# Hedgehog attention, Fourier mixing and an FFN in one kernel: the DFT by symmetry with folded channels, row-tiled projections, layer-norm scale applied after the FFN, DMA transposes

## The chip, the cores and the metric

The kernel runs on one core of a Trainium2 chip. The metric is device time in microseconds (us). Executions of one kernel lie within about 1% of each other. Where two kernels are compared, their runs were taken on the same chip in turn.

## The reference, cut to what matters

For each of 8 batches: linear attention with an exponential feature map, then the real part of a two-dimensional DFT as a mixing layer, then a layer norm and an FFN.

```python
def phi(x):
    proj = einsum('bhsd,df->bhsf', x, w_phi)               # 64 -> 128 features
    proj = proj - max(abs(proj), axis=-1)
    return concatenate([exp(proj), exp(-proj)], axis=-1)
kv  = einsum('bhsf,bhsd->bhfd', phi(k), v);  z = sum(phi(k), axis=2)
x   = einsum('bhsf,bhfd->bhsd', phi(q), kv) / (phi(q) . z + 1e-6)   # 8 heads of 576 x 64
x   = heads side by side                                   # 576 x 512 per batch
u   = x + real(fft(fft(x, axis=1), axis=2))
un  = (u - mean(u)) / sqrt(var(u) + 1e-6)
out = u + relu(un @ w_ch1) @ w_ch2                         # 512 -> 2048 -> 512
```

## The kernel before

Each batch has three stages, and each loop turn writes the attention of batch b+1 ahead of mixing and FFN of batch b. What is interleaved with what is fixed when the program is built: in the four steady batches from 255 to 590 us the trace shows the same TensorE order from the mixing's last product to the FFN's first, with the numerators (`psnum`) of two heads in each.

```python
# attention, per head h (pr = h // 2; rr = the 64 partitions of this head)
nc.tensor.matmul(psqh[:, 0:512], lhsT=wphi2[rr, :], rhs=QT[rr, pr, 0:512], start=True, stop=True)
...                                                   # and columns 512 to 640
nc.scalar.activation(out=QPh_p[:], in_=psqh[:, 0:640], func=AT.Exp, scale=1.0)
nc.scalar.activation(out=QPh_n[:], in_=psqh[:, 0:640], func=AT.Exp, scale=-1.0)
...                                                   # psqs, pskk: 5 matmuls each; max |.| of both
...                                                   # KPp, KPn: exponentials; VSCp, VSCn: values scaled
for fh in range(2):
    KP, VSC = (KPp, VSCp) if fh == 0 else (KPn, VSCn)
    c0 = 640 + fh * (D + 1)
    for jj in range(NSC):                             # NSC = 5 tiles of 128 rows
        nc.tensor.matmul(pskk[:, c0: c0 + D + 1], lhsT=KP[:, jj, :], rhs=VSC[:, jj, :],
                         start=(jj == 0), stop=(jj == NSC - 1))
...                                                   # kvh copy, psnum: 10 matmuls, X on VectorE

# mixing, after the column means (pmb) and sums (pcs)
for cc in range(NCC):
    for term, (MAT, DST) in enumerate([(CS_r, DT), (SS_r, ET)]):
        for kb in range(2):
            ...
            for js in range(NSC):
                nc.tensor.matmul(psD[:, 0:288], lhsT=XF[0:M, js, 128 * cc: 128 * cc + 128],
                                 rhs=MAT[0:M, js, 288 * kb: 288 * kb + 288], ...)
...                                                   # psu: 40 matmuls of 512 columns; U = psu + X
# layer norm: bn_stats and bn_aggr of the 5 row tiles, then
for g0, g1 in [(0, 3), (3, NSC)]:
    ...                                               # 1/sqrt(var) in rstd, by three Newton steps
    for kk in range(g0, g1):
        nc.scalar.activation(out=UN[0:M, kk, :], in_=U[0:M, kk, :], func=AT.Identity,
                             bias=nbias[0:M, kk: kk + 1], scale=rstd[0:M, kk: kk + 1])
        pUT = get_psumB().tile([128, 512], BF16, tag="pb", name="pUT")
        ...                                           # 4 transposes on TensorE into pUT
        nc.vector.tensor_copy(out=UNT[:, :, 128 * kk: 128 * kk + M], in_=pUT_v[:, :, 0:M])
...                                                   # FFN: psh, 128 matmuls of 288; pso, 80 of 512
nc.vector.tensor_tensor(out=OUT[0:M, :], in0=pso[0:M, :], in1=U[0:M, kk, :], op=ALU.add)
nc.sync.dma_start(out=out[b, 128 * kk: 128 * kk + M, :], in_=OUT[0:M, :])

# loop
for i, b in enumerate(batches):
    ...
    Xs[nb] = attention_core(nb, staged.pop(nb))       # nb: the next batch
    fft_ffn(b, Xs.pop(b))
```

## Time and profile before

| | before |
|---|---|
| time | 892.06 us (891.19 to 892.93) |
| TensorE busy | 673.9 us, 75% of the profiled span of 893.2 |
| VectorE, ScalarE, GpSimd busy | 467.0, 420.9, 110.2 us |
| first mixing stage begins at | about 136 us |
| a steady batch | 100.5 us, TensorE busy 82 |

The page of the kernel before gives the shares of the chain that ended last and, in 40 equal slices of the span, TensorE's busy tenths and the clock that it was granted, in tenths:

```profile
PE 64%; ACT 11%; DVE 8%; DMA 6%; SPq 6%; issue 2%; POOL 2%; DVEq 0%; ACTq 0%; POOLq 0%
...
PE   0112439795996699795996699787996799699887
...
PEclk9999999877996889877996889878996899689989
```

TensorE carries the chain, with a dip to 6 or 7 tenths in the middle of every batch, where its clock falls too. It lies between the mixing's last product and the FFN's first. The first fence has the last products, from the timeline; the second goes on in the chain in order of time (start, duration, what, number of instructions):

```profile
368.34 0.62 PE L390 MATMUL psu<-SDn_r,ET 128*64 128x512 bf16 x2
```

### The profile page before, as it was taken

How to read it: one execution, taken by the hardware profiler on the slowest of the kernel's cores; microseconds unless marked ns; L12 is line 12 of the kernel's file. 1: busy time of each engine (PE TensorE's matmuls, PEld its weight loads, DVE VectorE, ACT ScalarE, POOL GpSimd, SP SyncE). 2: the span in 40 equal slices, each digit the busy share in tenths (PEclk: the TensorE clock that was granted, in tenths of full speed). 3: DMA queues.
4: the chain of work that ended last, by engine and by line, in shares of the span. 5: the costliest groups of instructions: out<-in, count | busy, mean ns of one | idle time of the engine just before them, and what ended most of it. 6: DMA issues, size and time to landing. Idle time of an engine off the chain costs nothing.

```text
span 893.2 us, 13139 instructions
## 1 busy us (share of the span) xinstructions
PE 673.9 (75%) x5000; PEld 391.1 (44%) x5032; DVE 467.0 (52%) x1366; ACT 420.9 (47%) x886; POOL 110.2 (12%) x140
## 2 busy tenths in 40 slices
PE   0112439795996699795996699787996799699887
PEld 0002324463454445363454445364544545364463
DVE  8575635851477316951477316960577237833411
ACT  2599434373255425373155425373256606470270
POOL 8710140014000320014000320010000000000000
PEclk9999999877996889877996889878996899689989
DMA  9992190029100980029100980019100310001001
GB/s 99 147 196 19 32 107 1 1 30 110 54 1 1 93 82 18 1 27 113 54 2 1 90 85 18 1 26 73 43 1 1 59 54 1 1 1 48 6 1 53
DMA packets 164094, 39.15 MB, mean 44 GB/s; under 512 B 156864, under 2 KB 158912, under 8 KB 164032
## 3 DMA queue, kind: packets, MB, share of 16 engines
q0 software_dynamic: 115264, 18.39, 31.2%
q1 hardware_dynamic: 48768, 19.94, 10.9%
q8 instruction: 39, 0.64, 0.3%
q14 instruction: 23, 0.19, 0.1%
HBM read 36.77 MB, written 9.44 MB: 52 GB/s over the span
## 4 chain that ended last, share of the span: by engine, by line
PE 64%; ACT 11%; DVE 8%; DMA 6%; SPq 6%; issue 2%; POOL 2%; DVEq 0%; ACTq 0%; POOLq 0%
PE pso L486 16%; PE psh L474 12%; PE psD L361 12%; PE psu L385 4%; PE psu L390 3%; DMA VS<-in_v_dram 3%; SPq L195 3%; PE pskk L276 3%; SPq L196 3%; DMA QT<-QS 3%; PE pskk L235 3%; PE psqs L225 2%; PE psqh L210 2%; DVE MM L246 2%; PE psnum L290 2%
## 5 line engine op out<-in xcount | busy, mean ns | idle before, releaser
L474 PE MATMUL psh<-UNT,W1b 128*128 128x288 bf16 x1024 | 161.8, 320 | 16.7 <-ACT HT L481 16.7
L486 PE MATMUL pso<-W2b,HT 128*128 128x512 bf16 (+1 forms) x624 | 140.8, 380 | 0.8
L474 PEld LDWEIGHTS <-W1b 128*128 128x128 bf16 x1024 | 107.4, 109 | 57.9 <-issue 19.7
L481 ACT ACTIVATE HT<-psh 128x288 bf16<-128x288 f32 x256 | 97.9, 415 | 52.2 <-PE psh L474 46.0
L491 DVE TENSOR_TENSOR OUT<-pso,U 128x512 f32<-128x512 f32 (+1 forms) x40 | 27.6, 690 | 169.7 <-PE pso L486 169.7
L368 ACT CAST DT<-psD 128x288 bf16<-128x288 f32 x64 | 24.9, 404 | 155.2 <-PE psD L361 154.9
L486 PEld LDWEIGHTS <-HT 128*128 128x128 bf16 (+1 forms) x640 | 63.5, 100 | 73.5 <-issue 3.4
L276 PE MATMUL pskk<-VSCp,KPp 128*128 128x65 bf16 x320 | 23.4, 210 | 73.1 <-DVE VSCp L264 50.7
L361 PEld LDWEIGHTS <-XF 128*128 128x128 bf16 (+1 forms) x640 | 52.5, 98 | 55.3 <-issue 29.8
L243 DVE TENSOR_REDUCE MM<-psqs 128x5 f32<-128x640 f32 x64 | 52.7, 824 | 38.9 <-PE psqs L225 37.3
L220 ACT ACTIVATE QPhp<-psqh 128x640 bf16<-128x640 f32 x64 | 45.0, 704 | 53.3 <-PE psqh L214 48.5
L260 ACT ACTIVATE KPp<-pskk 128x640 bf16<-128x640 f32 x64 | 45.0, 702 | 52.2 <-DVE MM L246 39.0
L235 PE MATMUL pskk<-wphi,KT 64*128 64x128 bf16 x320 | 36.1, 248 | 39.8 <-DMA KT<-KS 38.1
L361 PE MATMUL psD<-CS_r,XF 128*128 128x288 bf16 (+1 forms) x320 | 62.8, 299 | 0.0
L361 PE MATMUL psD<-SS_r,XF 128*128 128x288 bf16 (+1 forms) x320 | 60.9, 298 | 0.0
L210 PE MATMUL psqh<-QT,wphi 64*128 64x512 bf16 x64 | 31.0, 484 | 39.4 <-DMA QT<-QS 29.7
L225 PE MATMUL psqs<-wphi,QT 64*128 64x128 bf16 x320 | 37.0, 258 | 25.8 <-ACT QPhn L221 21.1
L306 DVE TENSOR_TENSOR tmpg<-psnum,EE 128x325 f32<-128x325 f32 x64 | 31.7, 495 | 47.0 <-PE psnum L296 47.0
L276 PEld LDWEIGHTS <-KPp 128*128 128x128 bf16 x320 | 18.0, 107 | 87.0 <-ACT KPn L261 48.8
L246 DVE TENSOR_REDUCE MM<-pskk 128x5 f32<-128x640 f32 x64 | 52.0, 812 | 4.1 <-PE pskk L235 2.7
L173 POOL MEMSET VS<- 64x520 bf16 x8 | 4.5, 558 | 390.0 <-DVE VSCn L268 389.9
L225 PEld LDWEIGHTS <-QT 64*128 64x128 bf16 x320 | 24.5, 112 | 53.9 <-issue 33.8
(98 smaller groups left out, 1120.8 us busy)
## 6 DMA issues: line engine op xcount, KB each, us to landing
out_dram<-OUT SPq DMA_DIRECT2D x32, 256.0 KB, 2.0
QS<-in_q_dram POOLq DMA_DIRECT2D x32, 128.0 KB, 4.8
KS<-in_k_dram POOLq DMA_DIRECT2D x32, 128.0 KB, 4.7
VS<-in_v_dram POOLq DMA_DIRECT2D x32, 128.0 KB, 5.7
W1b<-in_moe_w_ch_dram POOLq DMA_DIRECT2D x1, 2048.0 KB, 14.6
W2b<-in_moe_w_ch_dram POOLq DMA_DIRECT2D x1, 2048.0 KB, 23.8
out_dram<-OUT SPq DMA_DIRECT2D x8, 128.0 KB, 2.3
QT<-QS SPq DMA_TRANSPOSE x40, 3.8
```

The source lines that it names most:

```text
L210: nc.tensor.matmul(psqh[:, 0:512], lhsT=wphi2[rr, :], rhs=QT[rr, pr, 0:512], start=True, stop=True,)
L220: nc.scalar.activation(out=QPh_p[:], in_=psqh[:, 0:640], func=AT.Exp, scale=1.0)
L225: nc.tensor.matmul(psqs_v[:, jj, :], lhsT=QT[rr, pr, 128 * jj: 128 * jj + 128], rhs=wphi2[rr, :], start=True, stop=True,)
L235: nc.tensor.matmul(pskk_v[:, jj, :], lhsT=KT[rr, pr, 128 * jj: 128 * jj + 128], rhs=wphi2[rr, :], start=True, stop=True,)
L243: nc.vector.tensor_reduce(out=MM[:, 0, :], in_=psqs_v, axis=AX.X, op=ALU.max, apply_absolute_value=True)
L246: nc.vector.tensor_reduce(out=MM[:, 1, :], in_=pskk_v, axis=AX.X, op=ALU.max, apply_absolute_value=True)
L260: nc.scalar.activation(out=KPp[:], in_=pskk_v, func=AT.Exp, scale=1.0)
L276: nc.tensor.matmul(pskk[:, c0: c0 + D + 1], lhsT=KP[:, jj, :], rhs=VSC[:, jj, :], start=(jj == 0), stop=(jj == NSC - 1),)
L361: nc.tensor.matmul(psD[:, 0:288], lhsT=XF[0:M, js, 128 * cc: 128 * cc + 128], rhs=MAT[0:M, js, 288 * kb: 288 * kb + 288], start=(js == 0), ...
L474: nc.tensor.matmul(psh[:, 0:288], lhsT=W1b[:, cc, 128 * hh: 128 * hh + 128], rhs=UNT[:, cc, 288 * hf: 288 * hf + 288], start=(cc == 0), st ...
L481: nc.scalar.activation(out=out_ap, in_=psh[:, 0:288], func=AT.Relu)
L486: nc.tensor.matmul(pso[0:M, :], lhsT=HT[:, hh, 128 * kk: 128 * kk + M], rhs=W2b[:, hh, :], start=(hh == 0), stop=(hh == NHH - 1),)
```

## The change

The intent was to take work from TensorE. The mixing of real rows has a symmetric result (row k at channel n equals row 576-k at channel 512-n), so half of the rows are computed and used twice; channels n and 512-n are added and subtracted first (`CE`, `CO`), so half of the channels are multiplied. Row 0 is subtracted from all rows, in place of the column means. Rows are loaded several to a descriptor, and projections go in pairs of 64-row tiles. The layer norm's mean is subtracted by GpSimd, a DMA transposes the result, and 1/sqrt multiplies the FFN's output, since ReLU lets a positive factor through. Cut to its core:

```diff
 # attention: 4 row tiles of 128 and, two heads to a tile, the last 64 rows
-                for jj in range(NSC):
-                    nc.tensor.matmul(
-                        pskk[:, c0: c0 + D + 1],
-                        lhsT=KP[:, jj, :],
-                        rhs=VSC[:, jj, :],
...
+                nc.tensor.matmul(
+                    kv[:, i, :], lhsT=K4[rr, pr, :], rhs=V4[rr, pr, :], start=True, stop=False
+                )
+                for j in range(4):
+                    nc.tensor.matmul(
+                        kv[:, i, :], lhsT=KP[:, h, j, :], rhs=VC[:, h, j, :],
+                        start=False, stop=(j == 3),
+                    )
...
 # mixing: row 0 subtracted, channels folded, half the rows
+        nc.vector.tensor_tensor(
+            out=XC[:, 0:4, 0:C], in0=X[:, 0:4, :],
+            in1=pm[:].unsqueeze(1).to_broadcast([128, 4, C]), op=ALU.subtract,
+        )
...
+        for sl in (slice(0, 2), slice(2, 4), slice(4, 5)):
+            for dst, op in ((CE, ALU.add), (CO, ALU.subtract)):
+                nc.gpsimd.tensor_tensor(
+                    out=dst[:, sl, :], in0=XC[:, sl, 0:256], in1=XC[:, sl, C:256:-1], op=op
+                )
...
+        for mt in range(2):
+            for src, mat, dst in ((CE, CS, DT), (CO, SS, ET)):
+                ps = pb.tile([128, NK], F32, tag="pb", name="psD")
+                for c in range(5):
+                    nc.tensor.matmul(
+                        ps[:], lhsT=src[:, c, 128 * mt:128 * mt + 128], rhs=mat[:, c, :],
...
 # layer norm
-                nc.scalar.activation(
-                    out=UN[0:M, kk, :], in_=U[0:M, kk, :], func=AT.Identity,
-                    bias=nbias[0:M, kk: kk + 1], scale=rstd[0:M, kk: kk + 1],
-                )
...
+            nc.gpsimd.tensor_scalar(
+                out=UN[0:M, c, :], in0=X[0:M, c, :], scalar1=mv[0:M, c, 0:1], scalar2=None,
+                op0=ALU.subtract,
+            )
+            nc.sync.dma_start_transpose(
+                out=UT[:, :, 128 * c:128 * c + M], in_=UN[0:M, c, :]
+            )
...
+                nc.vector.tensor_tensor(
+                    out=X[:, 2 + t, 1:C], in0=pu[:, C - 1:0:-1], in1=X[:, 2 + t, 1:C], op=ALU.add
+                )
...
 # FFN output
-            nc.vector.tensor_tensor(
-                out=OUT[0:M, :], in0=pso[0:M, :], in1=U[0:M, kk, :], op=ALU.add
-            )
+                nc.vector.scalar_tensor_tensor(
+                    out=O[0:M, :], in0=po[0:M, :], scalar=rs[0:M, c:c + 1], in1=U[0:M, c, :],
+                    op0=ALU.mult, op1=ALU.add,
+                )
...
 # loop
+    for b in range(B):
+        X = attention(b, loaded)
+        if b + 1 < B:
+            loaded = load(b + 1)
+        mixed = mixing(b, X)
+        if done is not None:
+            ffn(b - 1, *done)
+        done = mixed
+    ffn(B - 1, *done)
```

## The prediction

> **What bounds the kernel now.** I read the stages first, then the chain that ended last, then the groups. Stages (each engine's busy us in a stretch; PEclk is the granted clock, DMA the busy share of the 16 engines as the view scales it):
>
> ```profile
> 0.00:60.00 60.00, 6.67 (x46) 3.52 (x47) 43.95 (x133) 33.96 (x47) 37.66 (x51) 1.00 1.75 145
> 60.00:136.00 76.00, 29.13 (x268) 18.84 (x268) 41.26 (x119) 44.66 (x72) 15.42 (x19) 1.00 0.77 62
> ...
> 340.00:440.50 100.50, 82.19 (x627) 47.98 (x631) 52.68 (x155) 45.91 (x103) 13.09 (x16) 0.86 0.44 43
> ...
> 824.00:893.00 69.00, 60.09 (x347) 33.06 (x348) 17.19 (x56) 23.18 (x53) 0.00 (x0) 0.95 0.06 20
> ```
>
> So: 136 us pass before the first mixing stage; then a batch takes 95 to 102 us (here 340 to 440.5), with TensorE busy 82 of 100; a tail of 69. Inside that batch the chain is mostly TensorE in its own order:
>
> ```profile
> 412.54 1.90 ACT XB L325
> 415.32 4.87 PE psh L474 x28
> 420.45 10.74 PE pso L486 x49
> 431.25 3.09 PE pso L486 x13
> 434.33 1.29 PE pmb L330 x5
> 436.78 3.36 PE pso L486 x15
> 440.52 3.64 PE psD L361 x22
> ```
>
> and finer stretches show the two weak places, where TensorE waits for the attention's chain of VectorE and ScalarE (370 to 375), and for the next batch's transposes (397 to 413):
>
> ```profile
> 370.00:375.00 5.00, 1.33 (x20) 1.07 (x19) 4.75 (x24) 1.64 (x4) 0.00 (x0) 0.86 0.00 0
> ...
> 397.00:413.00 16.00, 8.32 (x77) 5.92 (x75) 3.94 (x13) 5.18 (x15) 6.40 (x8) 0.83 1.32 112
> ```
>
> The prologue is transfers (the DMA strip of the page stands at 9 tenths there; 156864 of 164094 packets under 512 B by the page) and table reloads: sines of the constants alternate with exponentials, and one head takes 20 us around 60 to 80 us.
>
> Dense work is best read at the end, with nothing beside it: psD 824.0 to 837.5 (13.5 us), psu to 846.2 (8.9), FFN 853.0 to 889 (36.0). These rows size the small work:
>
> ```profile
> L474 PE MATMUL psh<-UNT,W1b 128*128 128x288 bf16 x1024 | 161.8, 320 | 16.7 <-ACT HT L481 16.7
> ...
> L491 DVE TENSOR_TENSOR OUT<-pso,U 128x512 f32<-128x512 f32 (+1 forms) x40 | 27.6, 690 | 169.7 <-PE pso L486 169.7
> ...
> L243 DVE TENSOR_REDUCE MM<-psqs 128x5 f32<-128x640 f32 x64 | 52.7, 824 | 38.9 <-PE psqs L225 37.3
> L220 ACT ACTIVATE QPhp<-psqh 128x640 bf16<-128x640 f32 x64 | 45.0, 704 | 53.3 <-PE psqh L214 48.5
> ```
>
> (320 ns is a latency; the matmuls issue every 143 ns on average in that last FFN, 18.4 us for 128.)
>
> **What the Trainium skill says.** (1) "GPSIMD Engine Reference", section Performance versus the Vector engine: an fp32 two-operand add of 2048 columns takes 4497 ns on GpSimd and 2293 on VectorE. The trace agrees for VectorE: 495 ns at 325 columns and 690 at 512 give 1.04 ns a column, 2290 at 2048. It has no GpSimd arithmetic, so my GpSimd terms are estimates from this page: 2.2 ns a column plus some 0.1 us. (2) "TensorE: Matmul & The Clock Gate", Part 1: after idle windows of 3.4 us the array runs at half rate. The trace agrees: the ten psnum matmuls issue every 30 ns at 359 us, every 55 ns at 375 us (granted clock 0.50 from 375 to 380). (3) "ScalarE: Activation LUTs", What ACT_TABLE_LOAD costs: about 1283 ns; this trace has 1283.
>
> **The change part by part.** *Removed from TensorE per batch:* psD from 80 matmuls of 288 columns to 20 of 320: 13.5 to about 2.7 + 0.7 (the extra row px), psu from 40 to 12: 8.9 to 2.6. Mean and column-sum matmuls and transposes go (pmb 1.3, pcs 1.2, pUT about 2.2); one fp32 matmul for row 0 comes (some 1 us). Gain 13.5+8.9+4.7−7.0 = 20 us of TensorE. FFN (36) is unchanged; so are the 160 small kv and numerator matmuls. Projections stay 80 matmuls, in pairs of row tiles.
>
> *Prologue:* loads of 512 and 1024 B instead of 256; packets per batch fall from 13824 to 5632 (counted from the shapes), at the present 38.7 ns x packets / 16 engines that is 14 us. Only one batch is loaded ahead, and the constants need 28 VectorE steps instead of 126. But sines and exponentials still alternate in the built order. My sum for the first attention's end: data and transposes 20, key exponentials, sines and table loads 21, query part 12, heads 13: 66 us, against about 130.
>
> *The order is the risk.* The built order on TensorE is no longer interleaved. Each steady iteration is: heads(b), key projections(b+1), row 0 and mixing(b), FFN(b−1), query projections(b+1), heads(b+1). TensorE keeps this order, so it waits out each chain with only what stands before. I size the parts:
>
> - *D, query part after the FFN:* last output op 0.9; three reductions of 1024 columns at 1.22 (scaled from 824 ns at 640): 4.6; a small matmul and exponential 0.7; then eight exponentials of 1024 columns at 1.02 (from 704 at 640, 0.82 ns a column): 8.2, all ahead of the first kvh copy in ScalarE's order. 14 us, TensorE nearly idle, and cold.
> - *H, heads:* kv, copy, numerator, next kv: cold, 10 x 55 ns twice, 0.27 copy, 0.2 latency and two hand-offs: 1.65 x 8 = 13 us. VectorE's 1.2 a head fits below.
> - *B, mixing:* last tg, comb and rden with two key reductions between them 3.7; GpSimd's X 0.85; row-0 matmul 1.8; subtraction of 2048+512 columns on VectorE 2.9: centred rows at 9.3. GpSimd meanwhile has V4 twice, two load issues at 0.87 and four V products at 1.2 ahead of the fold, so it is free only at 12.4. Fold: copy 0.2, six sums 6.1, corner repair 1.6: 20.3. psD 4.6 (cold), copies 0.7, psu 4 to 5: FFN may start at 29.5.
> - *C, FFN:* 36, plus 2 because three psu buffers of the shared pool of three come free only as VectorE adds and normalises.
>
> Sum of a steady batch: 14+13+29.5+38 = 94.5, against 95 to 102. So the 20 us taken from TensorE come back as idle time of TensorE: I expect 2 to 7 us a batch from the steady state and the rest from the prologue.
>
> Whole: 66 + B(0) 30 + 5 (there no FFN hides the normalisation) + 7 x 94.5 = 662, less 7 for the last mixing (no next batch on GpSimd) + last FFN 36 + output tail 4 (as now, 889 to 893) = 796; call it 800.
>
> *LN scale on the output, DMA transposes:* UN's transposes leave TensorE, ScalarE and VectorE; five DMA transposes of 1.25 us issue each (present issue time of a 128x512) have a whole iteration to land. Key and query transposes follow the query part: 5.9 + 5.9 us of issue and some 2.5 to land, ending about 21 us after the FFN, while the heads end at 27. Hidden, with little to spare.
>
> **The rivals.** *A: TensorE stays the bound* and the time falls with its work: 20 x 8 = 160 plus the prologue's 60, about 680. For it: TensorE 75% busy, chain 64% TensorE. Against: the built order leaves nothing to fill the chains with. *B (mine): the chain of mixing and query part becomes the bound*, 800. *C: GpSimd is worse than its page*, or its port contends with VectorE: each 50% on its 17 us in B costs 8 us a batch, 860 or more. For it: GpSimd does some 30 us of arithmetic and 8 of issues per batch, where it had none; against: it is not on the path in C and D. *D: key transposes late*, so that key projections stand in front of row 0 and the mixing waits: perhaps 5 us a batch, 835. For it: this wait exists today (397 to 413).
>
> **Range and chances.** B's chains may overlap better (a warm array saves 2 us in H and 3 in B; shorter hand-offs): 740. C and D push to 860. I give 740 to 855; faster 0.94, same 0.04, slower 0.02: the prologue's 60 us alone is 7%, and the steady state would have to get 6 us a batch worse to cancel it down to 2%.
>
> **What would show it.** Right: first mixing at 60 to 75 us; TensorE busy below 65% of the span; per batch two holes, 12 to 16 us with ScalarE on exponentials (QPHP, QPHN) after the last pso, and 15 to 20 us with GpSimd on CE and CO before psD, with GpSimd on the chain that ended last at 10% or more; psf starting at a low clock. GpSimd's 512-column sum 1.1 to 1.3 us; the 1024-column exponential 1.0. Wrong: a batch below 85 us (the chains overlap, rival A), GpSimd sums over 1.7 us (C), or ps4 and psk waiting for KT (D). A prologue over 90 us would mean that table loads or the weights' transfer hold it.

## More of the kernel before

```profile
373.92 0.77 PE pskk L276 x10
...
381.21 0.75 PE pskk L276 x10
381.96 0.91 PE pUT L456 x7
...
386.67 4.76 PE psh L474 x22
```

From the end of `psu` at 369.0 to `psh` at 386.6 there are 17.6 us (17.6 to 17.9 in the steady batches), in which the chain is two heads' attention (the two `pskk` groups) and the normalisation. The expectations below call this gap 19 us; they took the last `psu` in the chain, at 367.6, for the last on TensorE.

## The result and the profile after

The changed kernel took **816.7 us** (813.86 to 819.55), against 892.06. Ratios here are the mean time of one kernel's runs over that of the other's runs of the same rounds, so not quite the ratio of the quoted medians: 0.9173, 95% interval 0.9065 to 0.9281. A second set of runs gave 815.69 against 889.14, ratio 0.9194 (0.9148 to 0.9241). Faster, by 8%, and inside the predicted 740 to 855.

The page after (engines busy, then the chain's shares, then the slices):

```profile
PE 546.9 (67%) x3992; PEld 314.6 (39%) x3992; DVE 303.8 (37%) x612; ACT 312.1 (38%) x654; POOL 316.1 (39%) x381
...
PE 47%; ACT 14%; DMA 12%; POOL 12%; DVE 11%; issue 2%; ACTq 0%; DVEq 0%; POOLq 0%
...
PE   0005654669765895769765896749946797649995
...
PEclk9999995569855897559955797559955698559999
```

TensorE lost 127 us of work, but the time fell by only 75. In two slices of each batch, some 40 us, its clock is now granted at 5 tenths, where before it rarely fell below 7. Busy time counts a slowed matmul longer, so it is no pure measure of work. The stages (the columns are as in the prediction) show a prologue and then batches of 92 to 94 us:

```profile
0.00:76.00 76.00, 10.84 (x113) 6.75 (x113) 27.99 (x62) 36.98 (x56) 35.27 (x63) 1.00 1.06 135
...
461.00:555.00 94.00, 68.56 (x501) 39.17 (x500) 36.11 (x73) 37.20 (x80) 36.86 (x43) 0.73 0.28 45
...
736.00:812.00 76.00, 65.89 (x408) 39.95 (x407) 13.65 (x30) 25.50 (x62) 6.67 (x5) 0.98 0.15 40
```

TensorE's idle time in a batch rose from 18 us to 25. The chain of one batch, in order of time, names the stretches: FFN to 494, query part to 509, heads to 525, mixing to 553:

```profile
464.00 12.90 PE psf L547 x104
476.90 10.37 PE pso L560 x48
...
488.08 8.04 DMA out_dram<-O
...
496.98 3.41 DVE MQ L324 x3
...
501.62 1.02 ACT QPHP L367
...
512.04 0.16 PE kv L374
512.20 0.34 PE kv L378 x4
...
530.34 2.08 PE pm L411 x2
...
537.75 1.18 POOL CE L426
538.92 1.14 POOL CO L426
...
549.60 2.81 PE pu L486 x12
...
552.80 0.61 PE psf L547 x4
```

Only psf, pso, psD and pu are dense TensorE work here. In the rest ScalarE (eight exponentials), the heads' hand-offs and GpSimd's fold follow each other.

### The profile page after: what moved, and what is told of

Same layout as the page of the kernel before. It is cut to its first block, busy times and chain, and to the rows that moved or that the text cites. A ratio compares the mean times of both kernels' runs of the same rounds, so it can differ in the third digit from the quotient of the medians. Undisturbed runs are those within 1.5% of the kernel's fastest.

```text
span 812.1 us, 10263 instructions
## 1 busy us (share of the span) xinstructions
PE 546.9 (67%) x3992; PEld 314.6 (39%) x3992; DVE 303.8 (37%) x612; ACT 312.1 (38%) x654; POOL 316.1 (39%) x381
## 4 chain that ended last, share of the span: by engine, by line
PE 47%; ACT 14%; DMA 12%; POOL 12%; DVE 11%; issue 2%; ACTq 0%; DVEq 0%; POOLq 0%
PE psf L547 16%; PE pso L560 10%; DMA out_dram<-O 8%; DMA KT<-KS 4%; ACT QPHP L367 4%; DVE MQ L324 4%; ACT QPHN L367 4%; POOL CE L426 3%; POOL CO L426 3%; PE pu L486 3%; PE kv L378 3%; PE psD L451 2%; PE pm L411 2%; DVE cb L399 1%; DVE O L566 1%
## 5 line engine op out<-in xcount | busy, mean ns | idle before, releaser
L547 PE MATMUL psf<-UT,W1b 128*128 128x288 bf16 x1024 | 131.5, 286 | 6.8 <-ACT HT L553 5.0
L553 ACT ACTIVATE HT<-psf 128x288 bf16<-128x288 f32 x256 | 105.2, 411 | 67.1 <-PE psf L547 50.4
L402 POOL TENSOR_TENSOR X<-cb,rd 128x320 f32<-128x320 f32 x64 | 46.3, 724 | 152.6 <-DVE rd L401 152.3
L473 POOL TENSOR_SCALAR UN<-X,MV 128x512 bf16<-128x512 f32 (+1 forms) x40 | 61.9, 1559 | 9.2 <-DVE MV L472 8.9
L387 PEld LDWEIGHTS <-QPHN 128*128 128x128 bf16 x320 | 34.6, 127 | 54.2 <-issue 54.2
L279 DVE TENSOR_REDUCE MK<-psk 128x8 f32<-128x1024 f32 x32 | 38.1, 1206 | 17.6 <-PE psk L275 17.6
L293 POOL TENSOR_TENSOR VCn<-VS,VCn 128x512 bf16<-128x512 bf16 x32 | 33.9, 1059 | 27.0 <-ACT VCn L289 25.8
L387 PEld LDWEIGHTS <-QPHP 128*128 128x128 bf16 x320 | 37.8, 133 | 3.5 <-issue 3.5
L324 DVE TENSOR_REDUCE MQ<-psq 128x8 f32<-128x1024 f32 x32 | 37.4, 1207 | 0.8 <-PE psq L317 0.8
L293 POOL TENSOR_TENSOR VCp<-VS,VCp 128x512 bf16<-128x512 bf16 x32 | 33.8, 1057 | 3.8 <-ACT VCp L289 3.8
```

What stands on the lines that cost most here:

```text
L293: nc.gpsimd.tensor_tensor(out=VC[:, hs, :, 0:D], in0=VS[:, hs, :].rearrange("p h (j d) -> p h j d", d=D), in1=VC[:, hs, :, D:D + 1].to_bro ...
L324: nc.vector.tensor_reduce(out=mv_, in_=psq[:], axis=AX.X, op=ALU.max, apply_absolute_value=True)
L387: nc.tensor.matmul(pn_[:, i, 65 * c:65 * c + 65], lhsT=QP[:, h, 128 * c:128 * c + 128], rhs=kvh[:, i, :], start=True, stop=True,)
L402: nc.gpsimd.tensor_tensor(out=X[:, :, D * h:D * h + D], in0=cb[:, :, 0:D], in1=rd[:].to_broadcast([128, 5, D]), op=ALU.mult,)
L473: nc.gpsimd.tensor_scalar(out=UN[0:M, c, :], in0=X[0:M, c, :], scalar1=mv[0:M, c, 0:1], scalar2=None, op0=ALU.subtract,)
L547: nc.tensor.matmul(ps[:], lhsT=W1b[:, cc, 128 * hh:128 * hh + 128], rhs=UT[:, cc, 288 * hf:288 * hf + 288], start=(cc == 0), stop=(cc == N ...
```

## The experiments

Unless said otherwise each has the changed kernel as its base, was timed in three rounds and gave right results. They ran with the kernel before beside them: `e1` to `e4` (before: 890.33 us), `a0`, `e5`, `e6` and `e7` (889.14), `e9` and `b1` (888.45), `b2` and `b3` (888.87). The base stands at 0.9194 of before.

### e1_fwd: the output write

The chain above has an output write of 8 us, and the last output of the FFN waits for it (a buffer of two). Its rows go out with an outermost dimension of 2. The Trainium skill, "DMA: Bandwidth & Descriptors", section "Why a DMA increments its semaphore by 16 and not by 1", says that the slowest dimension larger than 1 decides over how many engines a transfer is spread, at most 16. The trace agrees: about 50 GB/s in that write, 177 to 218 in the others, and from 488 to 496 us the packets took 11.0% of the 16 engines' time, which is 1.8 engines. The edit splits it in two writes of 64 rows each; it leaves out the reversal. Its output is wrong, which doesn't matter for the time.

```diff
-return [(slice(0, 128), r[:, ::-1, 3 - c, :])]
+return [(slice(64 * a, 64 * a + 64), r[a, :, 3 - c, :]) for a in range(2)]
```

> Wrong on purpose: the rows of the mirrored half are written in forward order, from two transfers of 64 rows instead of one whose outermost dimension is 2; same bytes. Theory (the outermost dimension of 2 keeps the write on two of the 16 engines): these writes land in 2 to 3 us instead of 8, the output operation no longer waits for them (40.6 us in 9 waits of the changed kernel become under 5), time 14 to 19 us shorter, 796 to 802. Rival (the write is slow for its strided rows, whatever the engines): landing stays over 6 us, time within 5 us of the changed kernel.

Measured 799.33 us (798.37 to 801.71), ratio 0.898 (0.8953 to 0.9007): 16 us less than the base's 815.69. The wait of `O` for the write all but goes (waits of the base, then of this run: us in total, times, longest):

```profile
DVE O L566 <- DMA out_dram<-O: 40.6, 9, 4.8
```

```profile
DVE O L566 <- DMA out_dram<-O: 2.7, 1, 2.7
```

The write's shape cost 2 us a batch. The edit takes the reversal of the rows away together with the dimension of 2; that it was the number of engines rests on the 1.8 engines above.

### e2_wlate: the FFN's weights behind the first two batches

In the prologue of the changed kernel the key transposes stand behind the 4 MB of FFN weights:

```profile
18.71 20.79 DMA KT<-KS
39.54 0.65 PE ps L254 x8
```

The edit issues the weights after the load of batch 1.

```diff
-load_ffn_weights()
 for b in range(B):
     X = attention(b, loaded)
     if b + 1 < B: loaded = load(b + 1)
+    if b == 0: load_ffn_weights()
```

> The FFN weights are loaded after the first attention and the second batch's loads instead of right after the first batch's loads. Theory (the weights' 4 MB hold back the first key and query transposes): the last key transpose lands before 25 us instead of 39.5, the first row-0 matmul starts at 72 to 80 us instead of 95.7, time 15 to 23 us shorter, 794 to 802. Rival (table loads and the exponentials bound the prologue): row-0 matmul still after 88 us, gain under 8 us. A third: the late weights delay the first FFN and nothing is gained.

Measured 800.23 us (799.32 to 801.34), ratio 0.8987 (0.8962 to 0.9012). The transposes now land at 22.1 us, and the first mixing product (`pm`, row 0) comes at 80.5 instead of 95.7:

```profile
13.28 8.81 DMA KT<-KS
...
22.13 0.63 PE psk L275 x7
```

So 15 of the 25 us by which the prologue missed the prediction were the weights' transfer.

### e3_order: the FFN written before the mixing

In the change, FFN(b-1) is written after mixing(b) and shares a pool of three PSUM buffers with it, so the builder can put none of it into the chains of heads and mixing. The edit writes FFN(b-2) ahead of mixing(b).

```diff
-    mixed = mixing(b, X)
-    if done is not None: ffn(b - 1, *done)
-    done = mixed
+    if b >= 2: ffn(b - 2, *mixed.pop(b - 2))
+    mixed[b] = mixing(b, X)
```

> Only the order of writing changes: FFN(b-2) is written between attention(b) and mixing(b), instead of FFN(b-1) after mixing(b), so the shared PSUM pool no longer puts the FFN behind the mixing and attention goes first in priority. Theory (the 20 us taken from TensorE were lost to chains that the order leaves uncovered): query part and heads, 30 us a batch, run beside the FFN; a batch falls from 93 to 70 to 80 us, time 690 to 730, TensorE over 74% of the span. Rival (the chains are the bound in any order, and FFN matmuls between them make them longer): a batch stays over 88 us, time over 780.

Measured **725.65 us** (721.71 to 726.52), ratio 0.814 (0.8103 to 0.8178). No instruction was taken from any engine, and 90 us went. TensorE is busy 71% of the span, short of the 74% expected. Its granted clock rose too, from 0.78 to 0.87, and the same matmuls were busy 512 us instead of 547; the run does not part this from the holes themselves, nor the shared pool from the order of writing. The stages show 82 to 84 us a batch while the next loads run and 71 us after them:

```profile
282.00:364.00 82.00, 62.16 (x484) 33.70 (x487) 39.40 (x70) 32.39 (x77) 38.78 (x45) 0.83 0.38 59
...
601.00:672.00 71.00, 60.09 (x421) 33.48 (x426) 26.66 (x62) 17.73 (x45) 21.43 (x24) 0.90 0.13 33
```

### e4_nok4 and e6_mask: the 64-row matmul in each head

A head of the changed kernel took 2.12 us, where the prediction had 1.65. Its ten `kv` matmuls mix a product over 64 rows of the array (L374) with four over 128 (L378), and those ten take 1.0 us. The Trainium skill, "TensorEngine Tiling (Array Packing)", Tiling Modes, Key Properties, says that switching the tiling mode drains TensorE. The first edit leaves the 64-row product out (**wrong on purpose**); the second keeps it, over all 128 rows with zeros in the half that belongs to the other head, at the price of a `V4` product twice as wide.

```diff
-kv[:, i, :], lhsT=K4[rr, pr, :], rhs=V4[rr, pr, :], start=True, stop=False     # e4: left out
+kv[:, i, :], lhsT=K4[:, pr, :], rhs=V4[:, e, pr, :], start=True, stop=False    # e6: zeros in V4
```

> Wrong on purpose: the two matmuls per head that add the last 64 keys (64 rows of the array instead of 128) are left out. Theory (going between 64-row and 128-row tiles drains the array, 0.33 us a head in the chain): a head falls from 2.12 to 1.7 to 1.8 us, 8 x 8 x 0.35 = 22 us, time 786 to 797. Rival (they cost only their place in the queue, 2 x 55 ns): 7 us, time 806 to 812.

> Correct this time: the last 64 keys of each head go through all 128 rows of the array, with zeros in the value rows of the other head; as many matmuls as before, none of them of 64 rows in the head loop. Theory (changing the tile size drains the array): a head falls from 2.12 to 1.75 to 1.85 us, 18 to 24 us less, but the wider V products cost GpSimd 0.9 us a batch in the chain, 7 us; net 10 to 17 us below the yardstick. Rival (the cost is the two matmuls themselves): the heads stay at 2.1 us and the time rises by up to 7 us.

Measured: without it 783.59 us (781.79 to 785.39), ratio 0.88 (0.8772 to 0.8827), a little under the range expected, with a head at 1.56 us; over 128 rows 797.68 (796.46 to 798.42), ratio 0.8974 (0.8944 to 0.9003). In the second the same ten matmuls, with the same number of columns, take 0.56 us instead of 1.02, and a head 1.67:

```profile
501.90 0.06 PE kv L379
501.95 0.22 PE kv L383 x4
502.17 0.06 PE kv L379
502.23 0.23 PE kv L383 x4
502.49 0.28 ACT kvh L388
```

This is what the page's drain would look like. It costs about 0.46 us a head, for four changes of mode. The profile models matmul ends, but the head's length does not rest on that: kvh to kvh fell from 2.12 to 1.67.

### a0_after: the base again

> The changed kernel once more, as a yardstick on the same chip as the other runs of this call: 812 to 820 us, ratio to before 0.91 to 0.92.

Measured 815.69 us (814.02 to 822.68), ratio 0.9194 (0.9148 to 0.9241).

### e5_ks4: a second buffer for the small key tile (a miss)

The waits list had GpSimd held 17.0 us in 5 waits at the load of `KS4`, until the key transposes had read the only buffer, with the fold behind it.

```diff
-KS4 = stage.tile([64, H, D], BF16, tag="KS4", name="KS4")
+KS4 = stage4.tile([64, H, D], BF16, tag="KS4", name="KS4")     # own pool, two buffers
```

> The tile for the last 64 key rows of a batch gets two buffers instead of one. Theory (GpSimd, in its own order, waits for the key transpose before it may issue the next load of that tile, with the last head's X behind it, 2.3 us a batch and 4% of the chain): that wait leaves the chain, 6 batches x 2.3 to 3 us, time 14 to 18 us shorter than the yardstick. Rival (the key transpose itself is late and only moves the wait to the key projections): under 5 us.

Measured 817.74 us (817.37 to 819.42), ratio 0.9206 (0.9181 to 0.9231): nothing. My theory fell. The wait shrank only to 13.6 us in 4, the key transpose of 2.3 us still stands in the chain of four turns (five in the base), and in the turn without it `X` comes after the `V4` products and the issue of a load of `VS` on GpSimd.

### e7_all: the corrections together

The late weights, the order, the mask, the small buffer, and the output written in place over `X`, which takes away the two-buffer wait with right results.

> Correct: late weights, FFN(b-2) between attention and mixing, output written in place (no output tile to wait for), two buffers for the last key rows, full-height last keys. Theory (the waits are independent and the order hides the chains): from 725 us of the order alone, 16 less for the weights, 10 to 14 a batch less where loads run (82 to 71 us a batch, 4 batches), little more for the rest: 645 to 685. Rival (once the FFN fills the chains TensorE is the bound and the removed waits were already hidden): 690 to 715.

Measured 685.78 us (685.02 to 686.59), ratio 0.7717 (0.7696 to 0.7739), between the two expectations: the parts do not quite add. Its trace showed one VectorE instruction on 5 columns, which takes 0.17 us elsewhere, lasting 4.60 us (VectorE and then GpSimd in order of time, two fences):

```profile
405.81 4.60 DVE L528 SCALAR_TENSOR_TENSOR ys<-ys,VE 128x5 f32<-128x5 f32 x1
410.44 0.17 DVE L532 SCALAR_TENSOR_TENSOR rs<-ys,yn 128x5 f32<-128x5 f32 x1
```

```profile
404.76 1.58 POOL L478 TENSOR_SCALAR UN<-X,MV 64x512 bf16<-64x512 f32 x1
406.29 1.07 POOL L298 TENSOR_TENSOR VCn<-VS,VCn 128x512 bf16<-128x512 bf16 x1
...
409.33 1.05 POOL L298 TENSOR_TENSOR VCp<-VS,VCp 128x512 bf16<-128x512 bf16 x1
```

It ends with the last of five GpSimd instructions that follow each other. The Trainium skill, "SBUF — State Buffer", section "SBUF: two separate sides", says that GpSimd and a VectorE operation with two SBUF inputs share a port pair that one of them locks for a whole instruction. This operation has two inputs in SBUF. It lies on the chain that ended last, as does another of them that lasted 2.68 us.

### e9_unv: the mean subtracted on VectorE

The base is e7_all, and this is the only further edit.

```diff
-nc.gpsimd.tensor_scalar(out=UN[0:M, c, :], ...)
+nc.vector.tensor_scalar(out=UN[0:M, c, :], ...)
```

> All corrections of e7_all, and the subtraction of the mean (UN, five of 512 columns a batch) on VectorE in place of GpSimd. Theory (contention): GpSimd's 1.56 us instructions stretch the small VectorE operations beside them from about 0.17 to 0.5 us and one to 4.6, and they keep the V products behind them; taking them away frees 7.8 us of GpSimd a batch and costs VectorE some 5 x 0.3 to 0.6 us. Expected 665 to 680, with the small Newton operations of VectorE back below 0.3 us in the mean. Rival (TensorE's order is all that is left; the stretched operations lie beside it): 683 to 690, nothing changes.

Measured **672.06 us** (671.28 to 676.95), ratio 0.7589 (0.7545 to 0.7633), the best of all, as the contention theory expected. The same subtraction costs a third (groups: busy us, mean ns; e7_all, then this one):

```profile
L478 POOL TENSOR_SCALAR UN<-X,MV 128x512 bf16<-128x512 f32 (+1 forms) x40 | 61.9, 1557 | 21.1 <-DVE MV L477 20.9
```

```profile
L478 DVE TENSOR_SCALAR UN<-X,MV 128x512 bf16<-128x512 f32 (+1 forms) x40 | 19.3, 482 | 0.0
```

No small Newton operation lasts over 0.18 us any more. The two stretched operations on e7_all's chain come to 7.2 us, about half of the 14 us gained. What the run does not separate is how much came from the freed port and how much from the 7.8 us of GpSimd a batch.

### b1_ln, b2_defer, b3_dmat: the layer-norm part alone

These have the kernel **before** as their base. The first takes the whole layer-norm part of the change and nothing else.

```diff
-UN = Identity(U * rstd - mean * rstd)  (ScalarE) ; 4 transposes (TensorE) ; copy (VectorE)
+nc.gpsimd.tensor_scalar(out=UN, in0=U, scalar1=mean, op0=ALU.subtract)     # per row tile
+nc.sync.dma_start_transpose(out=UNT[:, :, 128 * kk: 128 * kk + M], in_=UN[0:M, kk, :])
-OUT = pso + U
+OUT = pso * rstd + U
```

> The kernel before with one part of the change alone: GpSimd subtracts the mean, a DMA transposes the centred rows, the deviation is applied in the FFN's output; ScalarE's normalising, TensorE's twenty transposes and VectorE's copies go. If work taken from TensorE is what counts: 2 to 3 us a batch less, 865 to 880. If the wait counts, since in the order of before the FFN of a batch follows its normalisation at once and the five GpSimd subtractions (7.8 us) and the transposes' landing (2 us) then stand in front of it: 5 to 7 us a batch more, 925 to 950. The second is my theory: this part pays only where an FFN of another batch lies between.

Measured **790.87 us** (789.65 to 792.45), ratio 0.891 (0.8874 to 0.8946). Both my numbers were wrong. This one part of the change gains 98 us, more than the whole change. From the end of `psu` at 335.8 the FFN now starts after 7 us (6 in most batches), not 17.6:

```profile
337.65 1.57 POOL UN L411
339.24 3.47 DMA UNT<-UN
...
342.84 4.52 PE psh L463 x20
```

I had taken TensorE's order as given. But the built order is not the same: only one head's numerators stand between `psu` and `psh`, where before there were two. That the builder does this because the FFN's input is ready earlier is argued, not shown. From the first `psu` of one batch to that of the next it takes 88.3 us, where the batch shown of the kernel before takes 100.5, and 10.6 of these 12 us are the gap. TensorE's granted clock rose as well, from 0.90 to 0.96.

Two halves of the part tell which counts. One defers 1/sqrt but keeps ScalarE, TensorE's transposes and VectorE's copies; the other takes the DMA transposes alone.

```diff
 # b2_defer, inside the loop over kk, right after bn_aggr
+UN[kk] = Identity(U[kk] - mean)  (ScalarE) ; 4 transposes (TensorE) ; copy (VectorE)
-OUT = pso + U
+OUT = pso * rstd + U
```

```diff
 # b3_dmat, after the Newton steps as before
 UN[kk] = Identity(U[kk] * rstd - mean * rstd)
-4 transposes (TensorE) ; copy (VectorE)
+nc.sync.dma_start_transpose(out=UNT[:, :, 128 * kk: 128 * kk + M], in_=UN[0:M, kk, :])
```

> The kernel before with only the deviation deferred: ScalarE subtracts each row tile's mean as soon as that tile's statistics are there, the deviation is applied in the FFN's output; TensorE's transposes and VectorE's copies stay. Theory after the LN-only run (790.87, 97.6 us under before, where I had expected 925 to 950): what paid is that the FFN starts 6 us instead of 19 us after the last product of the mixing, because less of the next attention's chain stands in the built order between them. Here TensorE's order still has one and a half heads in that gap (two in before, under one with the LN-only change), so only part of it: 840 to 875. Rival, that the Newton steps behind the statistics (5.7 us in the trace of before) are all of it: 800 to 830.

> The kernel before with only the DMA transposes in place of TensorE's twenty transposes and VectorE's copies a batch; ScalarE normalises as before, after the Newton steps. TensorE's order keeps two heads between the last product of the mixing and the first FFN matmul. Theory: the gap stays near 19 us (2 us of landing in place of 1.3 of transposes and copy), gain only 2.2 us of TensorE work a batch: 865 to 890. Rival, that the transposes on TensorE (or their places in PSUM) were what held the FFN: 800 to 830.

Measured: the deferral alone 803.92 us (799.28 to 806.82), ratio 0.9017 (0.8967 to 0.9066), at what I had called the rival; the DMA transposes alone 900.41 (897.54 to 907.85), ratio 1.0131 (1.0075 to 1.0188), 1.3% longer, the same at the 2% mark. So deferring 1/sqrt is worth 85 of the 98 us, and my range for the transposes, 865 to 890, was missed. The chain of the deferral has a gap of 11 us (psu ends at 342.4):

```profile
349.82 0.75 PE pskk L276 x10
350.57 0.53 PE pUT L422 x5
...
353.09 0.60 PE psh L471 x2
```

What fills the gap is VectorE. The stretches below are the gaps of the kernel before, of the deferral and of the whole part (columns as in the prediction, VectorE's busy time the third), and VectorE is busy for 14.7, 10.4 and 6.2 us of them. Before, the last step (`X`) of three heads is among its work there; in the other two, of one.

```profile
369.00:386.60 17.60, 9.54 (x94) 6.97 (x94) 14.74 (x62) 10.13 (x19) 0.00 (x0) 0.63 0.01 1
```

```profile
342.40:353.00 10.60, 6.06 (x74) 4.25 (x72) 10.43 (x48) 6.18 (x12) 0.00 (x0) 0.66 0.00 0
```

```profile
335.80:342.80 7.00, 1.81 (x27) 1.24 (x27) 6.20 (x22) 1.56 (x3) 5.40 (x4) 0.80 0.30 60
```

The deferral's batch takes 85.0 us, 15.5 less than before, of which the gap explains 7. The list of TensorE's waits shows the rest: in 400 us of the kernel before there are these two, and neither is in the list of the deferral (over 360 us):

```profile
PE psqh L210 <- DMA QT<-QS: 23.4, 4, 6.6
PE psh L474 <- ACT HT L481: 11.4, 3, 3.8
```

They are 8 to 9 us a batch. The DMA transposes alone leave a gap of 18 to 19 us, as expected, with two heads still in it.

## Why the prediction was right, point by point

**The whole.** 800 predicted, 816.7 measured. The terms of the sum against the trace (prologue: end of the first batch's heads; the rest from the chain of the batch at 459 to 553 us):

| term | predicted | measured |
|---|---|---|
| prologue | 66 | 90.7 |
| C, FFN | 38 | 34.9 |
| D, query part | 14 | 14.8 |
| H, heads | 13 | 15.7 |
| B, mixing until the FFN may start | 29.5 | 28.0 |
| steady batch | 94.5 | 93.3 |

That the sum of 796 came within 16 us of the trace's 812 is in part luck: the prologue's 25 us too many met 8 us too few in the rest (the first turn 2, the steady batches with the last mixing 7 and the last two FFNs 4 too few, the output's tail 4.5 too many). The gain lies otherwise than forecast as well: of the 81 us between the two profiled runs, 36 come before the first mixing product (131.3 to 95.7 us), where 60 were forecast. The other 45 are 6.5 us a batch, within the 2 to 7 forecast.

**The signs.** Those seen: the two holes, and GpSimd with 12% of the chain. Those not seen: the first mixing product came at 95.7 us and not at 60 to 75, TensorE was busy 67% and not below 65%, and `psf` starts at full clock (1.00 from 553 to 556 us).

**Right: the order is the risk.** The claim that TensorE's saving comes back as idle time, because nothing is left to fill the chains with, is shown by e3_order: the same work in another order is 90 us shorter. It is only partly so: in the batch at 461 to 555 us, against that at 340 to 440.5 before, TensorE is busy 13.6 us less, of which 7 came back as idle time. Rival A's 680 was within reach, though not by the order alone: with it and four small corrections the kernel came to 685.78, and with one more to 672.06.

**Wrong: the prologue term.** It missed by 25 us, the one large error. "Data and transposes 20" left out that the weights' 4 MB are issued ahead of where the key transposes can land; e2_wlate shows 15 us of it. The other 9 to 10 us I did not split. The prediction had named this as its warning sign, for a prologue over 90 us.

**Mis-sized: H, 1.65 a head.** The hand-offs and the numerators were sized well; the ten `kv` matmuls were taken at 55 ns each and took 102 in the mean, from the change of mode. With it gone a head measured 1.67. (A slip without effect on this sum: 2.7 us for the new `psD` is too low, since 13.5 us scaled by matmuls and columns give 3.75.)

**Mis-sized: D.** It has the reductions and exponentials as predicted (in the chain 1.1 and 0.92 us each) and an unforeseen 2 us for the output write: the last `pso` ends at 494.3, and `O` starts at 496.2, when the write has landed. e1_fwd took 2 us a batch off.

**Right within a microsecond or three: B and C.** GpSimd's 512-column sum took 1.14 to 1.18 us where 1.1 to 1.3 had been said. Rival C (slow GpSimd or a fight for the port) has some truth: small VectorE operations were stretched (the one of L516 to 0.64 us in the median, where e9_unv has 0.17), but in the changed kernel beside the path of the steady batch; on the path it shows once the order is mended (e7_all and e9_unv). Rival D (late key transposes) came in small and by another way: the batch at 459 to 553 us has no transpose in its chain, but each of the five turns before it has one of 2.3 us (at 91.3, 153.8, 246.7, 339.2 and 431.5 us), for which GpSimd waited with `X` behind it, and not TensorE's key projections.

**Wrong by omission: the layer-norm part.** The prediction gave it 2.2 us of TensorE and called the rest hidden. For the changed kernel as it stands that may hold, since another batch's FFN lies between. But the prediction never asked what that part would do in the order of before. There it is worth 98 us alone. So all the rest of the change together, in the order it came with, costs about 25 us more than it saves, measured against that kernel (790.87 to 816.7), in spite of taking TensorE's busy time from 629 to 547 us. With its order mended the rest pays: 725.65.

**Open.** The last 9 to 10 us of the prologue; what the port contention by itself costs; and how the deferral came to close the second hole of the kernel before (the wait for query transposes), which the traces show but no run isolates. In the best kernel GpSimd's fold still holds TensorE's `psD`: 47.3 us of waits in all for the sums, the first thing to try next.

## What to carry to other kernels

Taking work from the busiest engine pays only if its instruction order leaves something to run while a dependent chain is waited out; look at where the next batch's dense work is placed, and at the buffers that tie it there, before counting saved matmuls. A scalar factor that commutes with the following layer, like a layer norm's deviation through a ReLU, is worth deferring for the wait it removes, even where it saves no work. A shorter chain can also move other instructions in the order that is built, so check the built order of a variant instead of reasoning with the old one.

## What the Trainium skill lacked or had wrong

- "GPSIMD Engine Reference", section 4.1: it calls one-input operations on GpSimd roughly line-rate. Here the subtraction of 512 columns with one tensor input and a mean per partition (float to bfloat16) took 1557 ns on GpSimd and 482 on VectorE, and on GpSimd it was slower than a two-input float sum of 512 columns (1140 to 1180). Its figure for two inputs, in section 3, agrees: some 2.2 to 2.3 ns a column.
- "TensorEngine Tiling (Array Packing)", Key Properties: says that a mode switch drains TensorE, but not what that costs. Here some 0.46 us for the four changes in a head, 18 us over the kernel when it was replaced (with the cost of the wider product) and 32 when it was left out.
- "SBUF — State Buffer", two separate sides: a lock for the whole instruction of the one that came first. Here a VectorE operation that takes 0.17 us lasted 4.6 us, to the end of the fifth GpSimd instruction in a row, so one instruction's length is no upper limit.
- "Perfetto Trace Analysis", Optimization Strategy, advises interleaving stretches with different limits, but neither it nor another page that I found says how much the built order alone can cost, or how to see that it is the bound: 90 us of 816 here, with the same instructions.
